# Scores of batch 0 from unsplit fp32 q and k, and the last stage's PSUM banks as one tile each

## The chip, the cores and the metric

One NeuronCore of a Trainium2 chip runs the whole program. The metric is the device time of one execution in microseconds (us). The engines are TensorE (PE), VectorE (DVE), ScalarE (ACT), GpSimd (POOL) and SyncE (SP, which only issues DMAs here); each takes its instructions in a fixed order and waits on semaphores for the others.

## The reference, cut to what matters

```
# q, k, v: (4, 12, 448, 64) float32
scores = matmul(q, k.transpose) / 8
scores = cap * tanh(scores / cap)
attn   = softmax(scores)
x = matmul(attn, v) -> (4, 448, 768)
# first MLP: h = relu(x @ w_in), u, v = halves of h, v normalised,
#            w_spatial applied over the rows, gated, @ w_out
# second:    theta = x @ w_theta; z = x cos(theta), x sin(theta)
#            y = w_tok_r @ zr + w_tok_i @ zi; u = x + y
out = u + relu(u @ w_ch)
```

## The kernel before

**Pairs of heads.** Attention runs over 4 batches and, in each, over 6 pairs of heads (p = 0 to 5). A pair's q and k are loaded row-wise, turned on PE by transposes into PSUM (`turn`, tile `tqk`), so that head 0 lies in partitions 0 to 63 (LO) and head 1 in 64 to 127 (UP), and copied out to SBUF. The 448 keys of a head are 64 tail keys and three blocks of 128. `scores(g)` makes four score tiles `sc` per pair: g = 0 is the 64 tail keys of both heads in one tile of 128 rows, g = 1 to 3 hold two blocks of 128 keys each. ACT applies tanh and exp to each (`et` for g = 0, `e` for the others), and PE sums exp times v into the PSUM banks `av` and `sum` (tile `acc`), one per head.

**Number formats.** A product of fp32r operands is one instruction and one record in the trace. To keep fp32 accuracy the kernel splits an operand into a high and a low fp32r part and adds products of the parts. For the scores of every batch, k is laid out as its high part in 64 partitions over its low part in the other 64 (`XA`, `XB`; `XH` and `XT` are further copies of the high part), and q as `y` (high) and `yl` (low), so one score block is two fp32r products of 128 rows, and the tail tile three: 15 per pair. A product of plain fp32 operands is written as one matmul, and in the trace it is two records. In batch 0 (`direct` in the code) the sums over v already use plain fp32 (`attend_1`, tiles `e`, `et` and `v`), in the other batches split operands.

**Batch 0, pairs 0 and 1** (`soon` in the code) load each head's q twice, side by side, so that the transposes deliver q of one head in all 128 partitions (`load_twice`, 12 transposes); the later pairs of batch 0 get the doubling of `y` by three DMAs from SBUF to SBUF (`y_odd`, `y_even`).

**Order.** Every step is an `op(engine, due, cost, f, r, w)`. The order in which the ops are issued is the hand-kept list `ORDER`, a permutation of all op numbers; the tile framework then adds the semaphore waits from the tiles that each instruction reads and writes.

**Around it.** While batch 0 runs, w_in (float64 words) is loaded and converted on ACT, DVE and POOL; the MLP stages of the earlier batch fill PE between the attention steps of the later ones. The last stage, the product with w_ch, is a seven-product (Strassen) scheme over pairs of batches: runs of three to nine products into one of six PSUM banks (`f_ps`), each then copied by ACT or added up by DVE (tile `p`), and transposed back (`o_ps`) for the store. The six banks are handed out in turn by `new_bank()`. Two come from the pool `ps_mm`; four are the halves of two tiles of 1024 words that the score tiles used before:

```
def open_bank(k):
    fin["s", k] = ps_s.tile([128, 1024], F32, tag="s", name="f_ps")
```

Before the first transposes PE runs 11 products on zeros, and 7 more after them (`warm_up`, tile `idle`).

Of the kernel before, what the change touches and what calls it, by code (L numbers as in the profile page):

```python
# [10 lines left out]
F32 = mybir.dt.float32  # L11
# [331 lines left out]
def attn_moe_moe2_kernel(ctx: ExitStack, tc: tile.TileContext, q, k, v, cap, w_in, w_sp, b_sp, w_out,  # L343
# [2007 lines left out]
```

## Time and profile before

| | |
|---|---|
| median of 3 runs | 763.88 us (762.16 to 765.02) |
| the profiled execution, its own time | 763.6 us |
| its span in the profile | 761.8 us |
| busy share of PE, DVE, ACT, POOL | 98%, 81%, 62%, 45% |

The span is what the trace covers; 1.8 us of the execution's own time lie around it. A busy PE is not PE at its peak: a record's duration has the way through the array in it and overlaps the next record, so the time that a product costs is read from the distance between the starts of neighbours.

### The profile page before, as it was taken

The numbers are of one execution on the slowest core, as the hardware profiler recorded it, in microseconds if no ns is written. First come the engines' busy times: TensorE is split into PE (matmuls) and PEld (weight loads), VectorE is DVE, ScalarE is ACT, GpSimd is POOL, SyncE is SP. The second block draws the span as 40 slices with busy tenths as digits, with TensorE's granted clock in tenths as the row PEclk, the third lists the DMA queues.
The fourth block names the chain that finished last, engine by engine and source line by source line (L and its number), as shares of the span: only waits on it lengthen the run. The fifth ranks groups of instructions, "written<-read, shape, count | busy, mean of one in ns | idle before, by whom it ended". The sixth has DMA issues, their size and how long they took to land.

```text
span 761.8 us, 11555 instructions
## 1 busy us (share of the span) xinstructions
PE 743.9 (98%) x3965; PEld 643.1 (84%) x3965; DVE 620.2 (81%) x992; ACT 476.0 (62%) x798; POOL 343.0 (45%) x464
## 2 busy tenths in 40 slices
PE   7999999999999999999999999999999999999997
PEld 4655678888888888887899999999999999888896
DVE  4969988798687978799987776899878877997865
ACT  4989878788779878896454644543514533553453
POOL 4889675544555465561100012232332422877650
PEclk9999999999999999999999999999999999999999
DMA  6677333242432541431343330011210000000135
GB/s 174 190 202 182 109 101 93 57 106 64 101 93 51 123 98 33 119 76 43 92 144 115 121 94 1 1 43 43 62 42 22 22 2 1 1 0 1 37 108 147
DMA packets 82062, 59.31 MB, mean 78 GB/s; under 512 B 47330, under 2 KB 75204, under 8 KB 82004
## 3 DMA queue, kind: packets, MB, share of 16 engines
q1 hardware_dynamic: 80100, 54.61, 27.1%
q0 software_dynamic: 1152, 3.64, 1.5%
q8 instruction: 31, 0.51, 0.3%
q10 hardware_dynamic: 752, 0.33, 0.2%
q14 instruction: 27, 0.22, 0.1%
HBM read 44.18 MB, written 5.62 MB: 65 GB/s over the span
## 4 chain that ended last, share of the span: by engine, by line
PE 72%; DVE 5%; ACT 2%; POOL 1%; issue 1%; DVEq 0%; POOLq 0%; ACTq 0%
PE ps_mm L404 16%; PE y_ps L404 12%; PE th_ps L404 12%; PE f_ps L404 10%; PE acc L404 7%; PE sc L404 5%; PE ps_sum L404 3%; PE ps_av L404 3%; PE o_ps L2172 1%; PE tqk L711 1%; PE x_ps L1624 1%; DVE ll L407 1%; DVE p L2152 1%; DVE s L995 1%; PE tok_ps L1500 1%
## 5 line engine op out<-in xcount | busy, mean ns | idle before, releaser
L404 PE MATMUL y_ps<-tok_h,zt 128*128 128x448 f32 x312 | 99.0, 368 | 0.1
L824 ACT ACTIVATE e<-e,cap_sb 128x896 f32<-128x896 f32 x72 | 74.8, 1043 | 1.0
L821 ACT ACTIVATE e<-sc,icap 128x896 f32<-128x896 f32 x72 | 72.1, 1005 | 4.7 <-PE sc L404 3.8
L407 DVE TENSOR_TENSOR ll<-e,hh 128x896 fp32r<-128x896 f32 x54 | 59.3, 1103 | 16.0 <-ACT hh L829 14.1
L404 PEld LDWEIGHTS y_ps<-tok_h,zt 128*128 128x128 f32 x312 | 58.6, 188 | 5.1 <-POOL zt L407 0.4
L404 PE MATMUL th_ps<-th_ah,x 128*128 128x256 f32 x288 | 57.4, 284 | 0.0
L404 PE MATMUL y_ps<-tok_l,zt 128*128 128x448 f32 x156 | 57.4, 368 | 0.0
L407 POOL TENSOR_TENSOR zt<-z,zt 128x1024 fp32r<-128x1024 f32 x12 | 29.6, 2470 | 59.2 <-ACT zt L1739 59.2
L407 POOL TENSOR_TENSOR x<-x,x 128x384 fp32r<-128x384 f32 (+1 forms) x15 | 18.5, 1242 | 74.0 <-ACT x L1565 65.1
L404 PE MATMUL f_ps<-x,S 128*128 128x448 f32 x216 | 49.8, 372 | 1.6 <-DVE p L2152 1.0
L1678 POOL TENSOR_SCALAR n<-n 128x512 f32<-128x512 f32 (+1 forms) x24 | 16.0, 669 | 76.8 <-DVE n L1675 76.8
L404 PE MATMUL ps_mm<-w_in_h,x 128*128 128x512 f32 (+1 forms) x132 | 47.8, 400 | 0.9 <-DVE gated L1256 0.8
L404 PE MATMUL ps_mm<-x,w_in_h 128*128 128x448 f32 x168 | 48.3, 368 | 0.0
L404 PEld LDWEIGHTS th_ps<-th_ah,x 128*128 128x128 f32 x288 | 46.8, 190 | 0.8
L404 PE MATMUL sc<-yl,XH 128*128 128x448 f32 x126 | 46.4, 368 | 0.0
L404 PEld LDWEIGHTS f_ps<-x,S 128*128 128x128 f32 x216 | 39.6, 188 | 6.3 <-DVE p L2152 1.6
L404 PE MATMUL f_ps<-x,a 128*128 128x448 f32 (+2 forms) x171 | 38.8, 362 | 2.3 <-DVE p L2152 1.7
L404 PE MATMUL acc<-ll,vh 128*128 128x448 f32 x108 | 40.1, 371 | 0.8 <-DVE ll L407 0.8
L1739 ACT CAST zt<-z 128x1024 fp32r<-128x1024 f32 (+2 forms) x36 | 24.3, 691 | 26.2 <-DVE z L1710 22.7
L404 PE MATMUL th_ps<-th_al,x 128*128 128x256 f32 x144 | 40.6, 282 | 0.0
L450 ACT ACTIVATE hb<-bits 128x384 f32<-128x384 f32 (+4 forms) x40 | 22.7, 567 | 27.6 <-DMA bits<-in_moe_w_ch_dram 15.5
L404 PE MATMUL acc<-hh,vh 128*128 128x448 f32 x108 | 39.6, 367 | 0.0
(328 smaller groups left out, 2366.1 us busy)
## 6 DMA issues: line engine op xcount, KB each, us to landing
y<-y SPq DMA_DIRECT2D x60, 112.0 KB, 2.2
bits<-in_moe_w_ch_dram SPq DMA_DIRECT2D x12, 384.0 KB, 3.1
out_dram<-o SPq DMA_DIRECT2D x23, 192.0 KB, 2.4
rq<-in_q_dram SPq DMA_DIRECT2D x33, 128.0 KB, 2.7
rk<-in_k_dram SPq DMA_DIRECT2D x11, 384.0 KB
r<-d SPq DMA_DIRECT2D x16, 224.0 KB, 3.8
rv<-in_v_dram SPq DMA_DIRECT2D x18, 192.0 KB, 2.6
w_in_bits<-in_moe_w_in_dram POOLq DMA_DIRECT2D x6, 512.0 KB, 4.6
```

The source lines that it names most:

```text
L404: nc.tensor.matmul(out=ps, lhsT=a, rhs=r, start=(first and i == 0), stop=(last and i == len(terms) - 1))
L407: (engine or nc.vector).tensor_tensor(out=o, in0=x, in1=f32(hi), op=ALU.subtract)
L450: nc.scalar.activation(out=hb(), in_=f32(words()[:, :, 1]), func=ACTF.Copy, scale=2.0 ** -112)
L711: nc.tensor.transpose(o, a, ident)
L821: nc.scalar.activation(out=st["e", g], in_=src, func=ACTF.Tanh, scale=icap)
L824: nc.scalar.activation(out=st["e", g], in_=st["e", g], func=ACTF.Exp, scale=cap_sb)
L995: nc.vector.reciprocal(out=st["s"], in_=st["s"])
L1500: nc.tensor.transpose(o, a[:, kk * 128:(kk + 1) * 128], ident[0:n, 0:n])
L1624: nc.tensor.transpose(o, x2(b, m)[:, p * 128:p * 128 + 128], ident)
L1678: nc.gpsimd.tensor_scalar(out=sd["n"], in0=sd["n"], scalar1=1.0, scalar2=-MAGIC, op0=ALU.mult, op1=ALU.add)
L1739: nc.scalar.copy(out=o, in_=a)
L2152: op("dve", t + 0.2, 0.54, lambda: TT(out=fin["p", o], in0=bank_of(kb), in1=fin["p", j], op=ALU.add), r=[kb, ("p", j)], w=[("p", o)])
```

## The change

Batch 0 no longer splits q and k. A pair's q and k are copied out of PSUM as plain fp32 into one tile `qk` (q by ACT, then k by DVE). A score block of one head is then one fp32 product over the 64 partitions of that head, and the two heads' products, on rows 0 to 63 and 64 to 127 of the array, stand next to each other in PE's order, each into its own bank. The tail tile g = 0 is one fp32 product of 128 rows, with k's tails on the diagonal blocks of a small tile `bd`. A group g now holds the same block of both heads, and the sums over v follow: `attend_1(g)` does both heads, the tail's two on 64 rows each. The doubled loads of q, the four fp32r parts, POOL's copies (`XH`, `XT`) and the doubling DMAs go away in batch 0. In the last stage each of the four banks is a tile of its own. `ORDER` is a new list throughout.

```
-        def load_twice(hd, u, queue):
-            queue.dma_start(out=twice()[0][hd][:, :, u], in_=q[b, h + hd, 0:384, :].rearrange("(r j) d -> r j d", j=3))
...
+        def load_head(name, src, hd, queue):
+            fresh(name, [128, 3, 2, 2, D])
+            queue.dma_start(out=raw[name][:, :, p % 2, hd], in_=src[b, h + hd, 0:384, :].rearrange("(r j) d -> r j d", j=3))
...
+            QS = ("sp", "act", "sp", "act") if p == 0 else ("sp",) * 4
+            QT = ("sp", "act") if p == 0 else ("sp", "sp")
...
+        if direct:
+            kqk = ring("l", 2)
+            kb = ("bd", p % 2)
+            def plain(n):
+                if n == 0:
+                    st["qk"] = att.tile([128, 2, S], F32, tag="l", name="qk", bufs=2)
+                (nc.vector.tensor_copy if n else nc.scalar.copy)(out=st["qk"][:, n], in_=st["qk"[n]])
+            def block(hd):
+                copy = nc.scalar.copy if hd else nc.vector.tensor_copy
+                copy(out=bd[HD[hd], p % 2, 64 * hd:64 * hd + 64], in_=st["k"][HD[hd], 0:64])
...
         def scores(g):
             ps = st["ps", g] = ps_s.tile([128, 1024], F32, tag="s", name="sc")
+            if direct:
+                q32, k32 = st["qk"][:, 0], st["qk"][:, 1]
+                if g == 0:
+                    products(ps[:, 0:S], [(bd[:, p % 2], q32)])
+                else:
+                    for hd in range(2):
+                        products(ps[:, 512 * hd:512 * hd + S], [(k32[HD[hd], 128 * g - 64:128 * g + 64], q32[HD[hd]])])
+                return
...
+        def attend_1(g):
+            for hd in range(2):
+                if g == 1:
+                    st["acc", hd] = ps_1.tile([128, S], F32, tag=("av", "sum")[hd], name="acc")
+                r = slice(0, 128) if g else HD[hd]
+                w = st["v"][r, 3 * hd + g - 1 if g else 6 + hd].rearrange("p a d -> p (a d)")
+                products(st["acc", hd], [(w, st["e", g][:, hd, :] if g else st["e", 0][r])], g == 1, g == 3)
...
-    def open_bank(k):
-        fin["s", k] = ps_s.tile([128, 1024], F32, tag="s", name="f_ps")
+    def open_banks():
+        ps_stack.close()
+        ps_f = ctx.enter_context(tc.tile_pool(name="ps_f", bufs=1, space=PSUM, side="right", reuse_waits="tile"))
+        for k in range(2):
+            for h in range(2):
+                fin["s", k, h] = ps_f.tile([128, 512], F32, tag="f%d%d" % (k, h), name="f_ps")
```

PE's order at its first scores, before: three products of the tail tile, four of g = 1, then the transposes of pair 1 (`rq`, `rk`, `tt` are the loaded q, k and tails).

```order
L404 MATMUL sc_211<-y_193,XT_100 128x448
L404 MATMUL sc_211<-y_186,XB_93 128x448
L404 MATMUL sc_211<-yl_191,XT_100 128x448
L404 MATMUL sc_218<-y_193,XA_91 128x448
L404 MATMUL sc_218<-yl_191,XH0_95 128x448
L404 MATMUL sc_218<-y_193,XB_93 128x448
L404 MATMUL sc_218<-yl_191,XH0_95 128x448
L694 MATMUL tqk_230<-ident_80,rq_122 128x128 x3
L695 MATMUL tqk_230<-ident_80,tt_124 128x64
L694 MATMUL tqk_231<-ident_80,rq_123 128x128 x3
L695 MATMUL tqk_231<-ident_80,tt_124 128x64
```

The same place in the changed kernel, and on to the first sums over v: `x2` on a row of `sc` or `acc` is the product of head 0 and that of head 1.

```order
L399 MATMUL sc_177<-qk_161,bd_97 128x448
L399 MATMUL sc_179<-qk_161 128x448 x2
L677 MATMUL tqk_184<-ident_80,rq_110 128x128 x3
L679 MATMUL tqk_184<-ident_80,tt_111 128x64
L680 MATMUL tqk_185<-ident_80,tt_111 128x64
L682 MATMUL tqk_185<-ident_80,rk_109 128x128 x3
L399 MATMUL sc_196<-qk_161 128x448 x2
L399 MATMUL sc_207<-qk_161 128x448 x2
L399 MATMUL sc_224<-qk_204,bd_97 128x448
L399 MATMUL acc_236<-e_194,v1_103 128x448
L399 MATMUL acc_238<-e_194,v1_103 128x448
L399 MATMUL acc_236<-et_182,v1_103 128x448
```

Seven fp32r products have become three fp32 ones, two of them on half of the rows; pair 1's transposes are eight in place of twelve. Farther on in batch 0, 64-row products stand mostly as a single couple between 128-row ones:

```order
L399 MATMUL acc<-e,v_104 128x448 x4
L399 MATMUL sc<-qk 128x448 x4
L399 MATMUL acc<-e,v_103 128x448 x2
L399 MATMUL sc<-qk,bd 128x448
L399 MATMUL acc<-et,v_103 128x448 x2
L399 MATMUL acc<-e,v_103 128x448 x2
```

Here the products of `sc<-qk` without `bd` and of `acc<-et` have 64 rows, the others 128.

The DMAs that SP issues first, before (pair 0's and 1's q, each twice, the tails, cap, k):

```order
L624 DMA tt<-in_k_dram 64x2x64
L617 DMA rq<-in_q_dram 128x3x64 x2
L620 DMA tt<-in_q_dram 64x2x64
L480 DMA cap_sb<-in_cap_dram 128x1
L617 DMA rq<-in_q_dram 128x3x64
L586 DMA rk<-in_k_dram 128x2x192
```

And in the changed kernel, where ACT's queue issues pair 0's two halves of k and k's tails, and POOL's queue, instead of three loads of tails, the first two loads of w_in:

```order
L611 DMA tt<-in_q_dram 64x2x64
L601 DMA rq<-in_q_dram 128x3x64 x2
L475 DMA cap_sb<-in_cap_dram 128x1
L601 DMA rk<-in_k_dram 128x3x64
L601 DMA rq<-in_q_dram 128x3x64
```

The one load of q that came fifth and belonged to pair 0 is gone; what follows cap now belongs to pair 1.

## Rows read from the trace of the kernel before

**Rows 1.** The page: busy time, share and records of each engine.
```profile
PE 743.9 (98%) x3965; PEld 643.1 (84%) x3965; DVE 620.2 (81%) x992; ACT 476.0 (62%) x798; POOL 343.0 (45%) x464
```

**Rows 2.** Windows: length, busy us (records) by engine, clock share, DMA share, GB/s.
```profile
0.00:12.34 12.34, 8.27 (x30) 3.35 (x31) 5.39 (x16) 2.76 (x4) 5.40 (x21) 1.00 0.53 126
12.34:81.01 68.67, 65.59 (x254) 41.00 (x254) 55.90 (x78) 62.08 (x89) 54.52 (x95) 1.00 0.72 194
81.01:86.00 4.99, 4.76 (x15) 3.80 (x15) 4.79 (x9) 3.25 (x7) 1.14 (x1) 0.66 0.49 138
...
654.83:762.00 107.17, 99.17 (x521) 87.55 (x519) 81.77 (x114) 47.97 (x117) 64.18 (x49) 1.00 0.20 52
```

**Rows 3.** Timeline of PE at the head: start, us, what, [idle before <-releaser].
```profile
7.61 0.52 PE L694 MATMUL tqk<-ident,rq 128*128 128x128 f32 x3 [1.56 <-DMA rq<-in_q_dram]
8.05 0.27 PE L695 MATMUL tqk<-ident,tt 64*128 64x64 f32 x1
8.26 0.55 PE L694 MATMUL tqk<-ident,rq 128*128 128x128 f32 x3
8.73 0.27 PE L695 MATMUL tqk<-ident,tt 64*128 64x64 f32 x1
8.74 0.27 PE L696 MATMUL tqk<-ident,tt 64*128 64x64 f32 x1
8.94 0.55 PE L698 MATMUL tqk<-ident,rk 128*128 128x128 f32 x3
9.32 1.67 PE L520 MATMUL idle<-zero 128*128 128x512 bf16 x7
12.34 0.47 PE L404 MATMUL sc<-y,XT 128*128 128x448 f32 x1 [1.34 <-POOL XT L773]
...
13.06 0.36 PE L404 MATMUL sc<-y,XA 128*128 128x448 f32 x1
13.26 0.36 PE L404 MATMUL sc<-yl,XH 128*128 128x448 f32 x1
```

**Rows 4.** Timeline of SP's queue at the head, the loads of q.
```profile
1.56 1.26 SPq L617 DMA_DIRECT2D rq<-in_q_dram  x2
...
4.17 0.54 SPq L617 DMA_DIRECT2D rq<-in_q_dram  x1
```

**Rows 5.** DMA queue of POOL: packets, MB, share of 16 engines' span.
```profile
q0 software_dynamic: 1152, 3.64, 1.5%
```

**Rows 6.** Timeline of PE at the first fp32 products, two records each.
```profile
17.18 1.67 PE L404 MATMUL acc<-e,v 128*128 128x448 f32 x4
18.68 0.92 PE L404 MATMUL acc<-et,v 128*128 128x448 f32 x2
```

**Rows 7.** Groups, 0 to 130 us: records (two per fp32 product), busy, mean ns | idle.
```profile
L404 PE MATMUL acc<-e,v 128*128 128x448 f32 x72 | 31.3, 546 | 0.7 <-issue 0.4 <-ACT e L824 0.2
```

**Rows 8.** Groups of ACT from 12.34 to 81 us, the four casts of q and k.
```profile
L766 ACT CAST XB<-tqk 64x448 fp32r<-64x448 f32 x6 | 3.2, 527 | 0.1
L765 ACT CAST XA<-tqk 64x448 fp32r<-64x448 f32 x6 | 3.1, 517 | 0.0
...
L735 ACT CAST y<-tqk 128x448 fp32r<-128x448 f32 x3 | 1.6, 531 | 0.0
L735 ACT CAST Y<-tqk 128x448 fp32r<-128x448 f32 x3 | 1.6, 524 | 0.0
```

**Rows 9.** The chain that ended last, in the last stage: start, us, what.
```profile
667.89 1.25 PE f_ps L404 x6
...
669.16 0.54 ACT p L2148
...
669.75 11.41 PE f_ps L404 x54
...
698.97 0.64 DVE p L2152
...
699.65 1.50 PE f_ps L404 x6
```

More of the change, by code (lines that the diff above doesn't have):

```diff
@@ L562, in attention @@
         h = 2 * p
-        q_ = p % 2 if direct else 0
-        xa, xb, xt, xh = XA[q_], XB[q_], XT[q_], XH[q_]
+        HD = (LO, UP)
         def kk(*names):
-            return [(n, q_) for n in names]
+            return [(n, 0) for n in names]
         FR = FRS[b > 0] if not (b == 0 and p == 1) else 5
@@ L686, in turn @@
         def turn():
-            if soon:
-                a, c = [ps_mm.tile([128, 512], F32, tag="mm", name="tqk") for _ in range(2)]
-                d = ps_1.tile([128, 512], F32, tag=("av", "sum")[p], name="tqk")
-                st["q"], st["q1"], st["k"] = a[:, 0:S], c[:, 0:S], d[:, 64:512]
-                rq_, tt_ = twice()
-                for hd, o in enumerate((a, c)):
-                    for j in range(3):
-                        nc.tensor.transpose(o[:, 128 * j:128 * j + 128], rq_[hd][:, j].rearrange("r u d -> r (u d)"), ident)
-                    nc.tensor.transpose(o[:, 384:448], tt_[:, hd].rearrange("r u d -> r (u d)"), ident[LO, LO])
-                nc.tensor.transpose(d[:, 64:128], raw["tt"][UP, p % 2].rearrange("r h d -> r (h d)"), ident[UP, UP])
-                for n in range(0, 384, 128):
-                    nc.tensor.transpose(d[:, 128 + n:256 + n], raw["rk"][:, p % 2, n:n + 128], ident)
-                return
             if direct:
@@ L702, in turn @@
                 st["q"], st["k"] = a[:, 0:S], c[:, 64:512]
-                to = [a[:, n:n + 128] for n in range(0, 512, 128)] + [c[:, n:n + 128] for n in range(0, 512, 128)]
+                for j in range(3):
+                    nc.tensor.transpose(a[:, 128 * j:128 * j + 128], raw["rq"][:, j, p % 2].rearrange("p h d -> p (h d)"), ident)
+                tails = raw["tt"][:, p % 2].rearrange("p h d -> p (h d)")
+                nc.tensor.transpose(a[:, 384:448], tails[LO], ident[LO, LO])
+                nc.tensor.transpose(c[:, 64:128], tails[UP], ident[UP, UP])
+                for j in range(3):
+                    nc.tensor.transpose(c[:, 128 * j + 128:128 * j + 256], raw["rk"][:, j, p % 2].rearrange("p h d -> p (h d)"), ident)
+                return
             else:
@@ L707, in turn @@
                 to = [a[:, n:n + 128] for n in range(0, 896, 128)]
-            src = [raw["rq"][:, j, p % 2] for j in range(3)] + [raw["tt"][:, p % 2]] * (2 if direct else 1)
+            src = [raw["rq"][:, j, p % 2] for j in range(3)] + [raw["tt"][:, p % 2]]
             src = [a.rearrange("p h d -> p (h d)") for a in src]
@@ L713, in attention @@
         ks = [ring("mm", 2), ring("mm", 2)] if direct else [ring("s", 2)]
-        if soon:
-            ks.append(("av", "sum")[p])
-        op("pe", t0 - FR - 6.5, 0.86, turn, w=ks,
-           r=[rk, rt] + [rq] * (not soon or p == 0) + ([("rq", p, n) for n in range(4)] + [("rt", p, n) for n in range(2)] + ([("xun", 3), ("xun", 4), ("xun", 5)] if p else [("xun", 2)])) * soon)
+        op("pe", t0 - FR - 6.5, 0.86, turn, w=ks, r=[(x, n) for x in (rk, rq, rt) for n in range(2)])
         if b == 0 and p < 2:
@@ L729, in new_y @@
         def new_y(hd):
-            st["y", hd] = Y[0][:, hd, :] if q_ else att.tile([128, S], F32R, tag="y%d" % hd, name="y")
+            st["y", hd] = att.tile([128, S], F32R, tag="y%d" % hd, name="y")
         def y_hi():
-            for hd in range(1 if soon else 2):
+            for hd in range(2):
                 new_y(hd)
             nc.scalar.copy(out=st["y", 0], in_=st["q"])
-        def new_yl():
-            if "yl" not in st:
-                st["yl"] = Y[1][:, 0, :] if q_ else att.tile([128, S], F32R, tag="yl", name="yl")
         def y_lo():
-            new_yl()
-            if soon:
-                difference(st["yl"][LO], st["q"][LO], st["y", 0][LO])
-                return
+            st["yl"] = att.tile([128, S], F32R, tag="yl", name="yl")
             difference(st["yl"], st["q"], st["y", 0])
-        def y_hi_1():
-            new_y(1)
-            nc.vector.tensor_copy(out=st["y", 1], in_=st["q1"])
-        def y_lo_1():
-            new_yl()
-            difference(st["yl"][UP], st["q1"][UP], st["y", 1][UP])
         def y_odd():
@@ L783, in x_hi @@
                                     scalar1=1.0, scalar2=0.0, op0=ALU.mult, op1=ALU.add)
-        for hd in range(2):
-            for n in range(2):
-                op("pool", t0 - FR - 2.3 + 0.5 * hd + 0.2 * n, 0.4 - 0.1 * n, lambda hd=hd, n=n: x_hi(hd, n),
-                   r=kk(("xah", "xbh")[(hd + n) % 2]), w=kk("xh%d%d" % (hd, n)), port=True)
-        op("act", t0 - FR - 5.2, ca, y_hi, r=ks, w=kk("y0") if soon else kk("y0", "y1"), banks=ks[:1])
-        op("dve", t0 - FR - 4.7, cd, y_lo, r=ks + kk("y0"), w=kk("yl"), banks=ks[:1])
@@ L791, in attention @@
-        if soon:
-            op("dve", t0 - FR - 4.9, 0.54, y_hi_1, r=ks, w=kk("y1"), banks=ks[1:2])
-            op("dve", t0 - FR - 4.4, 0.54, y_lo_1, r=ks + kk("y1"), w=kk("yl1"), banks=ks[1:2])
-        else:
+        if direct:
[8 more added lines that the diff above has]
+                copy(out=bd[HD[hd], p % 2, 64 * hd:64 * hd + 64], in_=st["k"][HD[hd], 0:64])
+            op("act", t0 - FR - 5.2, ca, lambda: plain(0), r=ks, w=[kqk] + ["begun"] * (b == p == 0), banks=ks[:1])
+            op("dve", t0 - FR - 4.8, cd, lambda: plain(1), r=ks + [kqk], w=[(kqk, 1)], banks=ks[1:])
+            for hd in range(2):
+                op(("dve", "act")[hd], t0 - FR - 4.9, 0.2, lambda hd=hd: block(hd), r=ks, w=[(kb, hd)], banks=ks[1:])
+        else:
+            op("act", t0 - FR - 3.9, ca, lambda: nc.scalar.copy(out=xa[LO, A0], in_=st["k"][LO]), r=ks, w=kk("xah"), banks=ks[-1:])
+            op("act", t0 - FR - 3.4, ca, lambda: nc.scalar.copy(out=xb[UP, A1], in_=st["k"][UP]), r=ks, w=kk("xbh"), banks=ks[-1:])
+            op("dve", t0 - FR - 3.4, cd, lambda: difference(xa[UP, A0], st["k"][LO], xa[LO, A0]), r=ks + kk("xah"), w=kk("xal"),
+               banks=ks[-1:])
+            op("dve", t0 - FR - 2.9, cd, lambda: difference(xb[LO, A1], st["k"][UP], xb[UP, A1]), r=ks + kk("xbh"), w=kk("xbl"),
+               banks=ks[-1:])
+            op("pool", t0 - FR - 2.8, 0.25, lambda: nc.gpsimd.tensor_copy(out=xt[LO, 0, 0:64], in_=f32(xa[LO, 0:64])),
+               r=kk("xah"), w=kk("xta"), port=True)
+            op("pool", t0 - FR - 2.6, 0.25, lambda: nc.gpsimd.tensor_copy(out=xt[:, 1, 0:64], in_=f32(xa[:, 0:64])),
+               r=kk("xah", "xal"), w=kk("xtc"), port=True)
+            op("pool", t0 - FR - 2.7, 0.25, lambda: nc.gpsimd.tensor_copy(out=xt[UP, 0, 64:128], in_=f32(xb[UP, 64:128])),
+               r=kk("xbh"), w=kk("xtb"), port=True)
+            for hd in range(2):
+                for n in range(2):
+                    op("pool", t0 - FR - 2.3 + 0.5 * hd + 0.2 * n, 0.4 - 0.1 * n, lambda hd=hd, n=n: x_hi(hd, n),
+                       r=kk(("xah", "xbh")[(hd + n) % 2]), w=kk("xh%d%d" % (hd, n)), port=True)
+            op("act", t0 - FR - 5.2, ca, y_hi, r=ks, w=kk("y0", "y1"), banks=ks[:1])
+            op("dve", t0 - FR - 4.7, cd, y_lo, r=ks + kk("y0"), w=kk("yl"), banks=ks[:1])
@@ L803, in scores @@
             ps = st["ps", g] = ps_s.tile([128, 1024], F32, tag="s", name="sc")
+            if direct:
[3 more added lines that the diff above has]
+                else:
+                    for hd in range(2):
+                        products(ps[:, 512 * hd:512 * hd + S], [(k32[HD[hd], 128 * g - 64:128 * g + 64], q32[HD[hd]])])
+                return
             if g == 0:
@@ L881, in attend_op, with attend_1_op @@
                 take(t, hd, 0)
-        def attend_1(hd, blocks, first, last):
-            if first:
-                st["acc", hd] = ps_1.tile([128, S], F32, tag=("av", "sum")[hd], name="acc")
-            terms = []
-            for g, i in blocks:
-                if g == 0:
-                    terms.append((st["v"][:, 6 + hd].rearrange("p a d -> p (a d)"), st["e", 0]))
-                else:
-                    j = 3 * hd + GROUPS[g][i][1]
-                    terms.append((st["v"][:, j].rearrange("p a d -> p (a d)"), st["e", g][:, i, :]))
-            products(st["acc", hd], terms, first, last)
-        def attend_1_op(t, hd, blocks, first, last):
-            bank = ("av", "sum")[hd]
-            op("pe", t0 + t, 4 * C * len(blocks), lambda: attend_1(hd, blocks, first, last),
-               r=[kv, (kv, hd)] + [K[g][0] for g, _ in blocks], w=[bank])
-            if last:
-                take(t, hd, 64 * hd)
+        def attend_1(g):
+            for hd in range(2):
+                if g == 1:
[3 more added lines that the diff above has]
+                products(st["acc", hd], [(w, st["e", g][:, hd, :] if g else st["e", 0][r])], g == 1, g == 3)
+        def attend_1_op(t, g):
+            op("pe", t0 + t, (8 if g else 4) * C, lambda: attend_1(g), r=[kv, (kv, 0), (kv, 1), K[g][0]], w=["av", "sum"])
         def take(t, hd, x0):
@@ L936, in attention @@
             op("pe", t0 + ts, n * C, lambda g=g: scores(g),
-               r=READS[g] + (["rv"] + [(x, i) for x in ("h", "l", "vl") for i in range(2)] if q_ else []), w=[ks])
+               r=READS[g], w=[ks])
             op("act", t0 + tt, 0.89 if g else 0.52, lambda g=g: tanh(g), r=[ks, "icap"], w=[ke])
@@ L943, in attention @@
                 if g == 2:
-                    attend_1_op(3.9, 0, ((1, 0), (1, 1)), True, False)
-                    attend_1_op(5.5, 0, ((0, 0), (2, 0)), False, True)
-                    attend_1_op(6.5, 1, ((0, 0), (2, 1)), True, False)
+                    attend_1_op(3.9, 1)
+                    attend_1_op(5.5, 0)
                 if g == 3:
-                    attend_1_op(7.7, 1, ((3, 0), (3, 1)), False, True)
+                    attend_1_op(6.5, 2)
+                    attend_1_op(7.7, 3)
+                    for hd in range(2):
+                        take(7.7, hd, 64 * hd)
                 continue
@@ L1326, in x2 @@
         return x2_tiles[b][:, m, :] if b < B - 1 else x2_tiles[b, m]
-    ATT = (["rv", "et", "ht", "lt", "sm"] + [(x, i) for x in ("rk", "rq", "tt", "vhl", "vl", "e", "h", "l") for i in range(3)] + ["c"]
+    ATT = ([((x, i), n) for x in ("rk", "rq", "tt") for i in range(2) for n in range(2)] + ["rv", "et", "ht", "lt", "sm"] + [(x, i) for x in ("rk", "rq", "tt", "vhl", "vl", "e", "h", "l") for i in range(3)] + ["c"]
            + [("xun", p) for p in range(NP)]
```

106 lines of the change are left out of this document (42 added, 64 removed), and 338 rows, old and new, of the table ORDER.

## The prediction

> **What bounds the kernel now.** The page comes first: PE is busy for 98% of the span, no other engine for more than 81% [rows 1]. A busy share alone does not prove a bound, so the stretches come next [rows 2]. Up to the first score, at 12.34 us, PE only turns pair 0 and runs products on zeros; most of batch 0's attention fills 12.34 to 81.01; in the next 5 us the granted clock is 0.66, that is part of the time at 1.2 instead of 2.4 GHz; the last stage fills 654.83 to 762. Between them PE is busy without gaps, so a microsecond of PE work taken out or put in there moves the end by as much. In batch 0 ACT is busy for 62.1 of 68.7 us, hardly less than PE.
>
> What a PE instruction costs is read from starts. An fp32r product of 448 columns takes 0.20 us (13.06 to 13.26) [rows 3], to three figures 0.203. A record of an fp32 product takes 0.375 us: four from 17.18 to 18.68 [rows 6]. A sum over v is two such records (72 and 24 of them for 48 products [rows 6, 7]), so an fp32 product costs 0.75.
>
> The sum is made against the profiled execution's own 763.6 us, 0.3 under the median; its last 1.8 lie outside the span and stay.
>
> **The head: -3.5 (bounds -4.1 and -2.8).** The first transposes wait for q [rows 3], whose last load is issued at 4.17 [rows 4]: 3.44 us from issue to use. In the changed kernel the last q load that they need is the second of the couple at 1.56, so issued at about 2.2; by the same 3.44 they start at 5.6. But POOL's queue now issues a 512 KB load of w_in ahead of that. q0's 1152 packets took 1.5% of 16 times 761.8 us, 0.159 us each [rows 5]; 128 of them over 16 DMA engines are 1.3 us if q waits for all. I take the middle, 6.2. The turn took 7.61 to 9.32 for twelve transposes; without one three and its tail (8.26 to 8.94 less what the UP tail shared) it is 1.05. Seven products on zeros follow, 1.5 us (1.67 less the 0.16 overlap of the last). So the first score starts at 8.8 instead of 12.34. ACT's and DVE's copies after the turn are hidden by those zeros: block and q on ACT, 0.25 (an estimate, half a 448-column cast) and 0.52 [rows 8], are over after 0.8 us, and k on DVE, which is queued behind ACT's q, is wanted one product later. On DVE the inversion of cap stands ahead of both copies; it waits for a load issued earlier than before. What was hidden by the old wait, the loads of pair 1, is issued until about 7.3 and usable by 10.7, when PE wants it.
>
> **The products: +2.3 (bounds -4.8 and +13.2).** Taken out: 15 fp32r products in each of 6 pairs, 90 times 0.203 = 18.3, and the 12 tail sums on 128 rows, 12 times 0.75 = 9.0; together 27.3. Put in: 6 tail scores on 128 rows, 4.5, and 24 couples of 64-row products (18 of scores, 6 of tail sums). No fp32 product on 64 rows stands in the trace. Three prices are possible. Nothing overlaps: four records, 1.5 us a couple, 36.0 in all. Everything overlaps: 0.75, 18.0. The two 64-row transposes that now stand next to each other, on lower and upper rows, start 0.01 apart, and the next instruction comes after 0.20 us as behind a lone one (0.21) [rows 3]: halves of the array do work at once. But they start in the order of the program, and there the lower half has two records before the upper half's first. If the second record of the lower half has to wait 0.375 for the first, and the upper half starts with it, a couple takes three slots, and couples next to each other share one. In PE's new order the 24 couples stand in 19 runs: 2 x 24 + 19 = 67 slots, 25.1 us. I take this one: 25.1 + 4.5 - 27.3 = +2.3.
>
> The Trainium skill ("TensorE: Matmul & The Clock Gate", part 3, The mechanism) says that products on different row groups overlap but start and end in program order; by that rule it is the staggered price. Its "TensorEngine Tiling (Array Packing)" (Theoretical Speedup) puts the gain for a contraction of 64 at up to twice, which is the full overlap below.
>
> **Changes between 128 and 64 rows: +5.7 (bounds 0 and 5.7).** Three transposes before a 128-row instruction take 0.38 (8.94 to 9.32), before a 64-row one 0.44 and 0.47; the 64-row one, of 64 columns and so worth about 0.06 beside 0.11 for 128, takes 0.20 [rows 3]. So going in costs 0.09, coming out 0.15, and the first weight load behind it 0.06 (0.38 against 3 x 0.11): 0.30 a run, 19 runs. The lower bound holds where PE waits for ACT at that point anyway.
>
> The Trainium skill ("TensorEngine Tiling (Array Packing)", Key Properties) says that a change of tiling mode drains TensorE; the rows agree, with about 0.3 us for in and out. Without such a cost the sum would be 5.7 lower.
>
> **Transposes: -0.2.** Pair 1's turn loses 0.65 like pair 0's; the four later pairs swap two full tails (0.22) for a 64-row couple (0.06 + 0.30), about +0.1 each.
>
> **Waits in batch 0: -4.0 (bounds 0 and -8).** From 12.34 to 81.01 PE's work adds up to 18.3 + 36.0 for scores and sums, 5.9 for the turns there, 2.2 for transposes of w_spatial: 62.4 of 68.7, so 6.3 us are waits. The slow clock behind them costs 0.34 of 5 us, 1.7 [rows 2]. ACT loses its casts, 9.5 us [rows 8], and gets 6 copies of 0.52 and 6 blocks of 0.25, 4.6: about 57 us of work. DVE loses as much and POOL nearly all of its part. PE's goes from 62.4 to about 70, so PE alone bounds this stretch and waits less. I take half: 3.2 of waits, 0.8 of clock.
>
> **The last stage: -4.5 (bounds 0 and -5.2).** Products stop at 669.14, ACT copies a bank out, and the next products start at 669.75, 0.04 us behind that copy; at 698.97 the same with DVE [rows 9]. There are five such places. Banks are handed out in turn, so the products that wait go to the other half of the two-bank tile, not to the bank that is read: the wait is for the tile. 0.61 to 0.70 in the chain, with the record's way through the array and an unhidden weight load about 0.9 by starts; 5 x 0.9. With a tile per bank it falls away. A sixth, at 754, may be one too (0.7).
>
> **Sum.** -3.5 + 2.3 + 5.7 - 0.2 - 4.0 - 4.5 = -4.2: 759.4 us. About 0.5%, 3.8 us, is what a measurement of this kernel can tell from no change, so "faster" is under 760.1 and "slower" over 767.7. By its bounds this case reaches from 754 to 764.
>
> **Rivals.**
> Full overlap, 15%: the upper half does not wait for the lower half's second record. For it: the 0.01 us above; against it: those transposes have one record each. Products cost -4.8 instead of +2.3, but PE then has about as much work as ACT and some 2 us of waits stay: 754.3.
>
> Products in series, 18%: the halves share the array for single-record transposes only, or the second weight load of the same half can't go ahead. +13.2 instead of +2.3, of which a microsecond hides in waits that go: 769.3, slower than before. It decides from about 1.22 us a couple on (1.05 on average above, plus 4.2 shared by 24).
>
> A wait is replaced, 12%: the last stage's waits are for the bank itself or for data, or the new order brings others, and the 4.5 don't come: 763.9, no change. For it: the same ACT copy also stands in the chain by order; against it: the six banks in turn.
>
> The staggered forecast keeps 55%. The range from 750 to 770 holds it with both neighbours. Faster takes somewhat over half of the forecast and all of the full overlap, 0.49; slower most of the serial case, 0.16; the rest is 0.35.
>
> **What would show it.** In the timeline of the changed kernel: the first score near 8.8 us; in a couple of `sc<-qk` four records with starts at about 0, 0.375, 0.38 and 0.75 (staggered), two at 0 (full), or 0.375 apart each (serial); a gap of 0.1 to 0.2 more than that on either side of a run; batch 0's last sum over v near 80 us, with ACT idler than before; no product of `f_ps` starting 0.04 us behind a copy of `p`. The prediction is wrong above all if a couple costs 0.75 or 1.5, or if the waits of batch 0 stay as they are.

## The result, and the profile of the changed kernel

The changed kernel takes 756.66 us (median of 4 runs, 756.37 to 757.26) against 764.13 of the kernel before: a ratio of 0.9907, 95% interval 0.9886 to 0.9927. The forecast was 759.4, the range 750 to 770. The profiled execution has a span of 755.1 us; the one before had 761.8, so 6.7 us are to be found. Of the ten executions of e1 below, one ran at a granted clock of 0.655 and took 1216.8 us; it is left out of e1's numbers.

The busy times of the page, and a windows view of the stretches that answer to [rows 1, 2] (length, busy us with records for PE, PEld, DVE, ACT, POOL, then granted clock, DMA share, GB/s):

```profile
PE 740.6 (98%) x3951; PEld 631.2 (84%) x3951; DVE 601.2 (80%) x979; ACT 471.2 (62%) x792; POOL 327.6 (43%) x419
```

```profile
0.00:14.20 14.20, 9.33 (x26) 3.92 (x27) 2.82 (x12) 2.02 (x3) 5.79 (x21) 1.00 0.71 190
14.20:82.87 68.67, 67.45 (x249) 29.80 (x248) 44.98 (x73) 59.36 (x86) 37.31 (x51) 1.00 0.60 163
82.87:87.86 4.99, 3.80 (x19) 2.73 (x18) 4.90 (x6) 3.40 (x7) 1.73 (x2) 1.00 0.24 66
650.07:755.00 104.93, 100.68 (x541) 91.82 (x539) 85.89 (x122) 50.18 (x121) 66.68 (x51) 1.00 0.20 53
```

The first row ends at the first score: 14.20 us, not 12.34 as before, and not 8.8 as forecast. The third row says that the slow clock behind batch 0 (0.66 in [rows 2]) is gone. The last row begins with the first product of `f_ps`. The same stretch of the kernel before is

```profile
650.65:761.80 111.15, 103.35 (x543) 91.39 (x541) 85.71 (x122) 51.27 (x124) 67.03 (x51) 1.00 0.19 50
```

so the last stage became 6.2 us shorter. In between, the end of batch 0 is found by counting back: each record of PE is taken at the usual distance between the starts of its shape, and where 640 us of such work remain, all of batch 0's own work is behind in both kernels. Before stands there at 101.01 us, the changed kernel at 102.77. From first score to that point it is 88.67 against 88.57; from there to the last stage 549.64 against 547.30. In all: +1.9, -0.1, -2.3 and -6.2. Each is a difference of two single executions.

**The head**, PE's timeline:

```profile
9.75 0.87 PE L677 MATMUL tqk<-ident,rq 128*128 128x128 f32 x3 [3.70 <-DMA tt<-in_k_dram]
10.55 0.37 PE L679 MATMUL tqk<-ident,tt 64*128 64x64 f32 x1
10.56 0.36 PE L680 MATMUL tqk<-ident,tt 64*128 64x64 f32 x1
10.85 0.90 PE L682 MATMUL tqk<-ident,rk 128*128 128x128 f32 x3
11.55 2.82 PE L515 MATMUL idle<-zero 128*128 128x512 bf16 x7
14.20 0.92 PE L399 MATMUL sc<-qk,bd 128*128 128x448 f32 x2
```

Against [rows 3] two things changed. The transposes start 2.1 us later, released by a load of k's tails, which ACT's queue had issued at 2.07 us, 7.7 us before:

```profile
2.07 0.65 ACTq L611 DMA_DIRECT2D tt<-in_k_dram  x1
```

And everything up to 13.7 us runs at half the speed: the seven products on zeros take 2.65 us from start to start of what follows (11.55 to 14.20), not the 1.5 that the forecast took from the kernel before; the turn takes 1.80 instead of 1.05. TensorE, which had stood still for 3.70 us (before for 1.56), ran at the lower of its two levels, 1.2 and 2.4 GHz: equal products on zeros start 0.427 us apart, and 0.216 in the kernel before.

POOL's timeline and the DMA view of the first 14 us (queue: packets, MB, share of 16 engines; issues: count, KB each, median us from issue to landing):

```profile
1.29 0.74 POOL L1019 DMA_DIRECT2D w_in_bits<-in_moe_w_in_dram  x1 [0.36 <-issue]
...
2.39 0.59 POOL L1019 DMA_DIRECT2D w_in_bits<-in_moe_w_in_dram  x1
```

```profile
q0 software_dynamic: 432, 1.57, 34.7%
...
rk<-in_k_dram SPq DMA_DIRECT2D x2, 96.0 KB, 6.4
```

In the kernel before POOL's queue has 0.14 MB in the same 14 us, and issues its first load of w_in at 12.22, behind copies that wait for ACT:

```profile
10.15 0.29 POOL L782 TENSOR_SCALAR XH<-XB 64x128 fp32r<-64x128 f32 x1 [5.38 <-ACT XB L766]
...
12.22 0.61 POOL L1038 DMA_DIRECT2D w_in_bits<-in_moe_w_in_dram  x1
```

Now it moves 1.57 MB, and the two loads of 96 KB of k on SP's queue, which belong to pair 1, take 6.4 us to land.

**Batch 0**, PE's timeline in two places (a product on 64 rows reads 64*128; each has two records):

```profile
24.60 1.02 PE L399 MATMUL sc<-qk 64*128 64x448 f32 x4
25.55 1.77 PE L399 MATMUL acc<-e,v 128*128 128x448 f32 x4
27.26 1.02 PE L399 MATMUL sc<-qk 64*128 64x448 f32 x4
...
39.05 1.77 PE L399 MATMUL sc<-qk 64*128 64x448 f32 x8
40.76 1.77 PE L399 MATMUL acc<-e,v 128*128 128x448 f32 x4
```

A lone couple, four records, takes 0.95 us from its start to the next (24.60 to 25.55); two couples next to each other take 1.71 (39.05 to 40.76). So a couple costs 0.75, what one product on 128 rows costs, and a run of them 0.20 more. Two products on 128 rows between two such runs take 1.71 instead of 1.50 (25.55 to 27.26), another 0.20. One run costs 0.40 in all. The four records of the first couple start at 15.048, 15.055, 15.528 and 15.535: the halves start together.

**The last stage**, whom PE waited for (line, engine waited for: us in total, times, longest), first before, then changed:

```profile
PE f_ps L404 <- DVE p L2152: 2.7, 5, 0.7
PE f_ps L404 <- ACT p L2148: 1.2, 2, 0.6
...
```

```profile
PE o_ps L2205 <- ACT o L2209: 0.5, 1, 0.5
PE f_ps L399 <- POOL x L402: 0.3, 1, 0.3
```

Before, products of `f_ps` waited seven times for a copy of `p` (the two copies have a line each); now none does.

### The profile page after: what moved, and what is told of

Same layout as the page of the kernel before. It is cut to its first block, busy times and chain, and to the rows that moved or that the text cites. A ratio compares the mean times of both kernels' runs of the same rounds, so it can differ in the third digit from the quotient of the medians.

```text
span 755.1 us, 11422 instructions
## 1 busy us (share of the span) xinstructions
PE 740.6 (98%) x3951; PEld 631.2 (84%) x3951; DVE 601.2 (80%) x979; ACT 471.2 (62%) x792; POOL 327.6 (43%) x419
## 4 chain that ended last, share of the span: by engine, by line
PE 85%; DVE 5%; ACT 3%; DMA 3%; POOL 1%; issue 1%; SPq 0%; DVEq 0%; ACTq 0%; POOLq 0%
PE ps_mm L399 20%; PE y_ps L399 13%; PE acc L399 12%; PE th_ps L399 12%; PE f_ps L399 9%; PE sc L399 8%; PE ps_sum L399 3%; PE ps_av L399 3%; PE tqk L691 2%; PE o_ps L2155 1%; DMA w_in_bits<-in_moe_w_in_dram 1%; PE x_ps L1605 1%; ACT e L808 1%; DMA y<-y 1%; DMA rq<-in_q_dram 1%
## 5 line engine op out<-in xcount | busy, mean ns | idle before, releaser
L402 DVE TENSOR_TENSOR ll<-e,hh 128x896 fp32r<-128x896 f32 x54 | 61.2, 1136 | 8.7 <-ACT hh L813 5.6
L895 DVE COPY s<-acc 1x448 f32<-1x448 f32 (+1 forms) x48 | 29.7, 618 | 14.0 <-ACT xun L887 6.6
L399 PE MATMUL sc<-yl,XH 128*128 128x448 f32 x108 | 39.5, 366 | 0.0
L399 PE MATMUL acc<-hh,vl 128*64 128x448 f32 x108 | 39.4, 364 | 0.0
```

What stands on the lines that cost most here:

```text
L399: nc.tensor.matmul(out=ps, lhsT=a, rhs=r, start=(first and i == 0), stop=(last and i == len(terms) - 1))
L402: (engine or nc.vector).tensor_tensor(out=o, in0=x, in1=f32(hi), op=ALU.subtract)
L895: nc.vector.tensor_copy(out=st["s"][64 * hd:64 * hd + n, :], in_=st["acc", hd][64 - x0:64 - x0 + n, :])
```

## The experiments

Each kernel was run beside the kernel before on the same chip; the ratio compares the two. The kernel before had medians from 763.57 to 765.74 us beside them, so kernels are compared by their ratios, and where the intervals of two overlap, the totals do not tell them apart. Those of e2 to e6 and e9 to e11 overlap that of the changed kernel; what is read from these runs against it rests on their traces, one execution each.

| | median us | ratio | 95% interval |
|---|---|---|---|
| changed | 756.66 | 0.9907 | 0.9886 to 0.9927 |
| e1, e10 banks alone | 759.48, 759.35 | 0.9952, 0.9940 | 0.9933 to 0.9971, 0.9921 to 0.9959 |
| e2 two-bank tiles | 758.48 | 0.9940 | 0.9919 to 0.9960 |
| e3 w_in held for pair 0 | 754.18 | 0.9881 | 0.9859 to 0.9903 |
| e4 20 zeros | 754.94 | 0.9895 | 0.9875 to 0.9915 |
| e5 w_in held for pairs 0, 1 | 754.63 | 0.9872 | 0.9848 to 0.9897 |
| e6 tails on 128 rows | 758.09 | 0.9922 | 0.9902 to 0.9943 |
| e7 couples twice, alternating | 768.18 | 1.0061 | 1.0042 to 1.0079 |
| e8 couples twice, in a row | 770.06 | 1.0079 | 1.0055 to 1.0104 |
| e9 v early | 755.00 | 0.9883 | 0.9862 to 0.9904 |
| e11 mixed | 757.80 | 0.9906 | 0.9869 to 0.9942 |
| e12 exp first | 754.98 | 0.9851 | 0.9826 to 0.9876 |

### The last stage: e1, e10 and e2

e1 gives the kernel before the four tiles of one bank, the whole order as it was (the two slots of the score tiles become pools of their own, so that each can be closed):

```
-        fin["s", k] = ps_s.tile([128, 1024], F32, tag="s", name="f_ps")
+        s_stacks[k].close()
+        ps_f = ctx.enter_context(tc.tile_pool(name="ps_f%d" % k, bufs=1, space=PSUM, ...))
+        for h in range(2):
+            fin["s", k, h] = ps_f.tile([128, 512], F32, tag="f%d%d" % (k, h), name="f_ps")
```

> The kernel before with nothing changed but the last stage's four banks, each a tile of its own. Theory (the five waits behind a copy of the other half of a two-bank tile are for the tile): the last stage loses them and nothing else moves. By the forecast's term 759.6 us (764.1 - 4.5); by what the changed kernel's trace shows between the same products, 6.1 us less in the last stage, 758.0. Rival (the wait is for the bank itself or for the copied data, and the gain seen in the last stage comes from the new order): 764, no change, and products of f_ps still start some 0.04 us behind a copy of p.

Measured: 759.48 us, 0.9952. e10 is the same kernel again, for a trace.

> The kernel of e1 once more, for its trace of the last stage. The five waits of 0.78 to 0.88 us behind a copy of the other half are gone if they were for the tile; some of the 8.6 us that PE loses after 650 us in the kernel before stay, since 3.9 us less were measured in e1, not 6.1: waits for a bank itself or for data, which the new order avoids.

Measured: 759.35, 0.9940. In e10's last stage PE waits for

```profile
PE o_ps L2184 <- DVE x L2174: 0.8, 1, 0.8
PE o_ps L2234 <- ACT o L2238: 0.6, 1, 0.6
```

The waits of `f_ps` for copies of `p` are gone, though the order is the old one: they were for the tile. From the first product of `f_ps` (653.01) to the end (759.98) it is 107.0 us against 111.2 before.

e2 is the other way round, the changed kernel with two-bank tiles:

```
-            for h in range(2):
-                fin["s", k, h] = ps_f.tile([128, 512], F32, tag="f%d%d" % (k, h), name="f_ps")
+            a = ps_f.tile([128, 1024], F32, tag="f%d" % k, name="f_ps")
+            for h in range(2):
+                fin["s", k, h] = a[:, 512 * h:512 * h + 512]
```

> The changed kernel, but the last stage's four banks are again the halves of two tiles of 1024 words. Theory (the tile is what is waited for): the five waits of 0.78 to 0.88 us come back, 4.2 us, so 760.9; if all that the last stage gained hangs on the tiles, 6.1 us, 762.8. Rival (the gain comes from the new order): 756.7.

Measured: 758.48, below both numbers of the theory and above the rival's. Its waits:

```profile
PE f_ps L399 <- DVE p L2136: 0.7, 2, 0.4
...
PE f_ps L399 <- POOL x L402: 0.5, 1, 0.5
```

Two waits for a copy of `p` come back, of seven. The stage takes 107.2 us (650.28 to 757.47). So either half is worth 4 us alone and 6.2 together: by these waits, the new order puts most of the products that would wait behind other work, and the tiles make the rest harmless. The expectation took the two as one. Which moves in the order do it was not tried.

### The head: e3, e4 and what became of the gain

e3 puts six reads of one number each ahead of POOL's first load of w_in, one of each load of pair 0; the load, which writes over them, has to wait:

```
+            if kk == 0 and half == 1:
+                for hd in range(2):
+                    r = slice(64 * hd, 64 * hd + 1)
+                    for x in (raw["rq"][r, 0, 0, hd, 0:1], raw["rk"][r, 0, 0, hd, 0:1], raw["tt"][r, 0, 0, 0:1]):
+                        nc.gpsimd.tensor_scalar(out=f32(st["b"][r, 0:1])[:, 0:1], in0=x, scalar1=1.0, scalar2=0.0, ...)
```

> The changed kernel, but POOL reads six single numbers of pair 0's loaded q, k and tails before it issues its first load of w_in, so that these loads of 512 KB start when pair 0 is in. Theory (pair 0's loads are late because the w_in loads share the DMA engines with them): the first transposes start near 6.2 instead of 9.75 us, the clock does not fall back in the shorter gap (0.11 us a transpose, 0.22 a product on zeros), the first score starts near 8.9 instead of 14.2, and the time is 756.7 - 5.3 = 751.4. Rival 1 (pair 0's and pair 1's own loads are in each other's way): transposes still after 9 us, 756.7. Rival 2 (w_in, which is now later by some 5 us, is wanted by the MLP at 86 us): the head gains 5.3 and the stretch up to 105 us gives back 2 to 5 of it, 754 to 756.

Measured: 754.18. The head did as the theory said; the total is the one of rival 2, but most of what is given back goes before 17 us, not at the MLP: record by record against the changed kernel's trace, PE is 5.5 us ahead at the first score, 2.7 at 15.7 us and 1.8 at the end. PE's timeline, and a window behind it:

```profile
5.84 0.85 PE L677 MATMUL tqk<-ident,rq 128*128 128x128 f32 x3
...
7.21 1.67 PE L515 MATMUL idle<-zero 128*128 128x512 bf16 x7
8.72 0.91 PE L399 MATMUL sc<-qk,bd 128*128 128x448 f32 x2
...
12.59 0.27 PE L679 MATMUL tqk<-ident,tt 64*128 64x64 f32 x1 [1.52 <-DMA tt<-in_q_dram]
```

```profile
13.30:16.60 3.30, 3.30 (x10) 1.17 (x8) 2.97 (x6) 2.12 (x4) 2.55 (x8) 0.52 0.51 114
```

The first score stands at 8.72, 5.5 us earlier, and the zeros take 1.5 us: with w_in out of the way the loads of pair 0 land where the forecast had them (5.84, forecast 6.2), so their lateness was w_in's doing; pair 1's two loads of k that took 6.4 us to land take 3.0 here. But w_in now goes in front of pair 1: its q tail is 1.52 us late, and behind that stop the granted clock is 0.52, 1.2 GHz nearly throughout, for 3.3 us.

e4 leaves the loads and changes only the warm-up, `warm_up(20, ...)` instead of `warm_up(11, ...)`:

> The changed kernel with 20 instead of 11 products on zeros ahead of the first transposes. They do nothing for the output. Theory (TensorE is at 1.2 GHz from 9.75 to 13.7 us because it stood idle from 6.05 to 9.75): the zeros reach up to 8 or 9.7 us, the transposes start at 9.75 as before but at full speed, 1.05 us for the turn and 1.5 for the seven zeros behind it instead of 1.8 and 2.65; the first score near 12.3 instead of 14.2; 756.7 - 1.9 = 754.8. Rival (the speed there does not hang on what TensorE did before): 0.21 us a transpose as now, 756.7.

Measured: 754.94, where the theory said 754.8. Record by record against the changed kernel's trace, PE is 2.2 us ahead at the first score and 1.9 at the end. The transposes still wait for a load, and run at full speed:

```profile
9.43 0.52 PE L677 MATMUL tqk<-ident,rq 128*128 128x128 f32 x3 [1.75 <-DMA tt<-in_k_dram]
...
10.47 1.67 PE L515 MATMUL idle<-zero 128*128 128x512 bf16 x7
11.98 0.92 PE L399 MATMUL sc<-qk,bd 128*128 128x448 f32 x2
```

So of the 5.4 us by which the head missed the forecast, lateness is 3.5 (9.75 instead of 6.2) and the clock 1.9.

e5 also reads a number of each load of pair 1 before w_in goes, and sets pair 0's v before that:

> As the kernel that held the first loads of w_in back, but POOL reads a number of each load of pair 1 too, and sets pair 0's and pair 1's constant parts of v before that; so the loads of w_in start near 11 us. Theory (what the 5.5 us at the first score lost again in e3 was pair 1: its q tail landed late behind w_in, PE stood still for 1.7 us in the middle of pair 1's turn and then ran 3 us at half the clock, 1.3 us): pair 1's turn runs through, no granted clock under 1 up to 20 us, and the time is 754.2 - 3.0 = 751.2. Rival 1 (ACT bounds the first 20 us, PE would wait for it there): the first score near 8.7 again, but the sum stays at 753.5 to 754.2. Rival 2 (w_in is late for the MLP): waits between 78 and 105 us grow, over 754.2.

Measured: 754.63 (with pair 0's constant parts of v alone moved, not pair 1's), by the ratio not to be told from e3, so the 3 us of the theory did not come. Rival 2's reason is not there either: the stops from 78 to 105 us are those of the changed kernel. Pair 1's turn runs through and the first score is at 8.31; then

```profile
26.07 3.20 PE L399 MATMUL acc<-e,v 128*128 128x448 f32 x4 [1.19 <-issue]
```

This view names no releaser. Pair 1's loads of v had all landed by 24.7 us, so they were not it. DVE was: PE's new sum needs the bank that DVE's first copy `s<-acc` empties, and that copy ends at 25.97, PE's wait at 26.01. It stood behind conversions of w_in, whose load was late. DVE's timeline:

```profile
22.93 0.43 DVE L448 TENSOR_SCALAR w_in_f<-w_in_bits 128x512 uint32<-128x512 uint32 x1 [1.75 <-DMA w_in_bits<-in_moe_w_in_dram]
...
25.35 1.26 DVE L895 COPY s<-acc 1x448 f32<-1x448 f32 x2
```

The products behind it run at half speed again. e9, whose expectation takes v for the reason, brings v's loads forward:

> As e5, but POOL also sets pair 1's constant parts of v before it issues w_in, and SP issues pair 1's loads of v ahead of pair 2's q and k. Theory (in e5 the sums of pair 1 waited 1.2 us at 26.1 us for v, whose loads stood behind POOL's memsets and those behind a conversion that waits for w_in; the stop was followed by 4 us at a lower granted clock, 2.2 us): both go, 754.6 - 3.4 = 751.2. Rival (ACT, 57 us of work in batch 0, bounds the stretch once the head is short): PE waits for ACT in other places, 753 to 754.6.

Measured: 755.00, near the rival's range. With v early the stop at 26 us is still there, though shorter, with DVE's copy named, and no slow clock follows; a new one is at 57 us. Timelines of PE, ACT and the weight loads (PEld), and a window of the DMA engines' share (next to last column):

```profile
26.33 1.74 PE L399 MATMUL acc<-e,v 128*128 128x448 f32 x4 [0.47 <-DVE s L895]
```

```profile
57.13 0.67 ACT L445 ACTIVATE w_in_bits<-w_in_bits 128x512 f32<-128x512 f32 x1 [1.91 <-DMA w_in_bits<-in_moe_w_in_dram]
57.71 1.02 ACT L808 ACTIVATE e<-e,cap_sb 128x896 f32<-128x896 f32 x1
```

```profile
59.33 1.02 PE L399 MATMUL acc<-e,v 128*128 128x448 f32 x2 [1.62 <-DMA w_sp_n<-in_moe_w_spatial_dram]
```

```profile
59.33 0.30 PEld L399 LDWEIGHTS acc<-e,v 128*128 128x128 f32 x2 [2.35 <-ACT xun L887]
```

```profile
16.00:18.00 2.00, 2.00 (x7) 0.60 (x6) 2.00 (x4) 2.00 (x3) 1.25 (x3) 1.00 1.32 249
```

For PE's stop the view names a load of w_spatial, which these sums do not read. For the weight load in front of them it names ACT's copy `xun<-acc` (58.76 to 59.28), which empties their bank. That copy stands behind an exp (57.71 to 58.73), and the exp behind a conversion of w_in whose load is 1.91 us late. e11 tries a middle way, w_in held for pair 0 alone and the loads of pair 1 in another order:

> As e3 (the first loads of w_in wait for pair 0 alone, so they start near 8 us instead of 10.6 in e9), with pair 1's tails moved ahead of its q and k in SP's queue, both pairs' constant parts of v set before w_in, and pair 1's v ahead of pair 2's q and k. Theory (from e3, e5 and e9: what the head gains is given back where something of pair 1 or 2 is late, and near 57 us, where ACT's exp stands behind a conversion that waits for a load of w_in; the later w_in starts, the longer): pair 1's turn without a stop, the wait at 57 us under 1 us instead of the 1.9 of e9, 752.5 to 753.5. Rival (the DMA engines are full up to 25 us whatever the order, so each order makes something late): 754 to 755 as e3, e5 and e9.

Measured: 757.80, with runs from 753.61 to 760.05: outside both ranges, though by the ratio not to be told from e3. Late loads are the rival's reason; now it is pair 1's q:

```profile
13.19 0.52 PE L677 MATMUL tqk<-ident,rq 128*128 128x128 f32 x3 [2.78 <-DMA rq<-in_q_dram]
```

e12 takes e9 and lets ACT do the exp first (ops 102 and 103, which follow the conversion on DVE, also move behind two others):

```
-... 197, 101, 251, 252, 221, 223, 220, 257, 224, 222, 253, 402, ...  # 101: the conversion, 251: the exp
+... 197, 251, 252, 221, 223, 220, 257, 224, 222, 253, 101, 402, ...
```

> As e9, but one conversion of w_in on ACT and its two successors on DVE stand four and one places later: ACT first does the exp of pair 4's last score group, the two copies out and the next tanh, and only then the conversion whose load was 1.9 us late at 57 us. Theory (PE's stop of 1.97 us at 57 us in e9 is that exp, queued behind a conversion that waits for a DMA): the stop goes, nothing else on PE moves by as much, 755.0 - 1.9 = 753.1. Rival (PE waits there for something else, or the conversion is wanted soon after on DVE and POOL): 755, with a stop of the same size within the next 30 us.

Measured: 754.98, the rival's number, though by ratio the lowest of all kernels here, 0.9851, with an interval clear of the changed kernel's; it overlaps that of e9. In its trace the stop at 57 us is gone, as the theory says:

```profile
26.85 3.33 PE L399 MATMUL acc<-e,v 128*128 128x448 f32 x4 [0.90 <-DVE s L895]
...
59.24 1.77 PE L399 MATMUL sc<-qk 64*128 64x448 f32 x8
60.94 1.40 PE L399 MATMUL acc<-e,v 128*128 128x448 f32 x3
```

1.70 us for the eight records, with nothing behind. In exchange this execution waited at 23.93 us for a tail of pair 2 (1.20 us) and at 26.85 for DVE's copy (first line), and ran at a granted clock of 0.81 on average from 22 to 40 us. e3, e5, e9, e11 and e12 together: the head's 5 us can be had, but while the DMA engines are this busy between 12 and 22 us (0.95 to 1.36 in e9), in each order tried some load is late, or a copy or exp stands behind a conversion whose load is late. The stop costs its own length and, in e3, e5, e11 and e12, the clock behind it.

### The products: e6, e7 and e8

e6 sums the tail keys over all 128 rows, `r = slice(0, 128)`, where the other head's half of v is zero:

> The changed kernel, but the sums over v of the tail keys use all 128 rows of et and of v, whose other half is zero: 12 products of 128 rows instead of 6 couples of 64, the same result. Theory (a couple costs as much as one product, 0.75 us, and a run of 64-row products 0.37 us for going in and out): 6 x 0.75 = 4.5 more and 5 of the 19 runs fewer, 5 x 0.37 = 1.85 less: 756.7 + 2.65 = 759.3. Rival 1 (the change of rows costs nothing of its own): 761.2. Rival 2 (a couple costs 1.5, its halves one after the other): 0 - 1.85, 754.8.

Measured: 758.09. In its trace, counted as above from the first score to the point with 640 us of work left, batch 0 is 2.1 us longer than in the changed kernel (105.43 - 14.75 = 90.68 against 88.57). By runs of 0.40, which the trace gives, theory says 4.5 - 5 x 0.40 = 2.5; the rivals say 4.5 and -2.0. The total is up by 1.4 only (within the noise), since a stop of 1.4 us that the changed kernel has at 552.3 us is not in e6's trace. Theory holds.

e7 and e8 issue each score couple twice:

```
-                    for hd in range(2):
+                    for hd in (0, 1, 0, 1):   # e8: (0, 0, 1, 1)
                         products(ps[:, 512 * hd:512 * hd + S], ...)
```

> The changed kernel with each of its 18 score couples issued twice, head 0, head 1, head 0, head 1, into the same banks; the result is that of the second. Theory (full overlap, 0.75 us a couple): 18 x 0.75 = 13.5 more, 770.2. Rival (halves in series, 1.5): 27 more, 783.7.

> The same doubled products, but in the order head 0, head 0, head 1, head 1. Theory A (each half of the array works off its own queue, so products need not alternate): 13.5 more, 770.2, and records of the two heads start together. Theory B (only neighbours in PE's order overlap, here the second and the third): 3 x 0.75 instead of 0.75 a group, 27 more, 783.7, with starts of head 0 alone, both, head 1 alone.

Measured: 768.18 and 770.06, 11.5 and 13.4 us over the changed kernel, where full overlap says 13.5 and series 27. PE's timeline at the first group, of e7 and of e8:

```profile
15.29 1.77 PE L399 MATMUL sc<-qk 64*128 64x448 f32 x8
16.99 0.55 PE L677 MATMUL tqk<-ident,rq 128*128 128x128 f32 x3
```

```profile
14.72 1.78 PE L399 MATMUL sc<-qk 64*128 64x448 f32 x8
16.44 0.55 PE L677 MATMUL tqk<-ident,rq 128*128 128x128 f32 x3
```

Four products take 1.70 and 1.72 us, in either order. If only neighbours overlapped, e8's group would take three times 0.75 and more. Its eight records start in four pairs 0.014 us apart, so the upper half starts with the lower; the first pair, in a window from 14.7 to 14.75 us:

```profile
14.72 0.65 PE L399 MATMUL sc<-qk 64*128 64x448 f32 x2
```

Theory A holds: the halves of the array do not wait for each other's turn in PE's order, at least not within four products.

## Why the forecast came out, and which of its steps failed

The direction and the size came out (759.4 against 756.66), but by luck: the products came 7.1 us lower than forecast and the head 5.4 higher, and most of that cancels. By its own sign its mechanism failed: it was to be wrong above all if a couple cost 0.75, and a couple does. In us:

| step | forecast | measured |
|---|---|---|
| head, to the first score | -3.5 | +1.9 |
| products of batch 0 | +2.3 | -4.8 |
| changes between 128 and 64 rows | +5.7 | +7.6 |
| transposes, waits and clock of batch 0 | -4.2 | -2.9 |
| from there to the last stage | 0 | -2.3 |
| last stage | -4.5 | -6.2 |
| sum | -4.2 | -6.7 |

**The head failed as a step.** The forecast priced POOL's load of w_in at 1.3 us at most, its packets spread evenly over the engines [rows 5], and let SP's loads of q take the 3.44 us of before. What the transposes waited for was another load, k's tails on ACT's queue, 7.7 us after its issue, and e3 shows that w_in is the reason: without it the first score stands at 8.72, where the forecast had 8.8. Why w_in was there: in the kernel before, the loads stand behind copies on POOL (`XH`, `XT`) that wait for ACT, and that is what held them until 12.22 us. The change removed the copies, and the wait with them. The forecast saw one load move and priced its bytes. Two are issued by 2.39 us, 2.5 us at its own price, and e3's transposes start 3.9 us earlier (5.84 against 9.75). The second miss is the clock: the transposes and zeros ran at 1.2 GHz, and e4, in which nine more products on zeros shorten the standstill before them from 3.70 to 1.75 us, shows that 1.9 us hang on that.

**The products failed as a step, the other way.** The forecast let the upper half wait for the lower half's second record, a couple for three slots. It takes two: 24 x 0.75 = 18.0, and with 4.5 for the tail scores, less 27.3, that is -4.8, the rival of full overlap. The sentence that failed is that halves start in program order. The Trainium skill ("TensorE: Matmul & The Clock Gate", part 3, The mechanism), by whose rule it was the staggered price, does not agree with these fp32 products: e8's group would have to start its upper half behind both products of the lower, and it starts 0.014 us after the first record. Its "TensorEngine Tiling (Array Packing)" (Theoretical Speedup), up to twice for a contraction of 64, does agree: 0.75 for two on 64 rows, as for one on 128.

**The changes of rows were right in kind, mis-sized by a third:** 0.40 a run, 19 runs, 7.6, where the forecast read 0.30 from transposes [rows 3]. e6 bears it out. That takes back all that the products gained and more.

**Waits of batch 0:** no run measures them; the row is what is left of the -0.1 of this stretch, -0.1 + 4.8 - 7.6 = -2.9, with the transposes in it. The slow clock of [rows 2] did go; but 4 us of stops remain or are new, two of them at 84.7 and 95.1 us (1.35 and 0.99 us over the usual distance), behind DVE's work on w_spatial and on exp. Half of the waits was a choice; it was somewhat too much.

**Between batch 0 and the last stage** the forecast had nothing. The new order lost six stops there (3.6 us in the kernel before) and has three others (2.5 us); the rest are small ones. The border to batch 0 is a choice, too: counted at about 147 us in place of 101, this row is -0.4 and batch 0's stretch -2.0. No run took these apart.

**The last stage: right in kind, and in size for the part it named.** The forecast took 4.5 for the tiles; e1 and e10 measure 3.7 and 4.6 (0.48% and 0.60% of 763.6 and 764.4), and the stage in e10's trace is 4.2 shorter. The other 1.6 to 2.5 come from the order of the last stage, which the forecast took as unchanged, and which alone would be worth as much as the tiles (e2).

## What to carry to other kernels

When a change removes work, ask what stood behind that work on its engine and ran late because of it: a large load that starts ten microseconds earlier can take the bandwidth of the small loads that start the kernel. When a load is moved back, ask what stands on each engine behind the instruction that waits for it. Two fp32 products on 64 rows of the array cost here as much as one on 128 (0.75 us), but each run of them costs 0.40 for going in and out, so put them in long runs. Two banks that are handed out separately should be two tiles; otherwise a product waits for a copy of its neighbour.

## What the runs showed of the hardware that was not expected

A row of the granted clock says nothing of the time before the trace's first entry. In the changed kernel the transposes and zeros from 9.75 us run at half speed, and the row reads 1.00:

```profile
9.75:13.70 3.95, 3.95 (x14) 2.07 (x15) 1.16 (x4) 0.74 (x2) 1.71 (x7) 1.00 0.71 202
```

The trace's record of the granted clock has its first entry, 1.00, at 13.86 us, and the view takes the time before as 1.00. In the kernel before the first entry is at 6.76, and there too the zeros ahead of it start 0.427 us apart. In e6, whose head is nearly the same, it is at 4.54, and the stretch from 12 to 14 us reads 0.50. So at the head the distance between the starts of equal products (0.427 or 0.216 us for one on zeros) is the sign to go by.

How long PE stands still does not alone decide whether the clock falls. In e3 (1.52 us), e5 (1.19), e11 (2.78) and e12 (1.20) the granted clock went to 0.50 within about 2 us of the stop's end, for 3 to 7 us. After 1.56 us in the kernel before and 1.75 us in e4, both ahead of the first transposes, and after 1.62 us at 57 us in e9, it did not.
